# First MLP's late part: three tiles of 512 tokens become two of 768, one of them with block sums for both weights

## The chip, the cores and the metric

The kernel runs on one core of one Trainium2 chip. The metric is device time in microseconds (us), the median of three timed runs. The traced execution has a time of its own, which stands beside its span.

## The reference, cut to what matters

Windowed attention (4 batches, 8 heads, 576 positions, head size 64), then two MLPs over the 2304 tokens of its output, with 512 model columns and 2048 hidden columns, all in float32:

```
x  = attention(q, k, v)                      # (2304, 512); first 4 heads: window of 32, last 4: every 4th of 128
h  = x @ moe_w_in;   r = max(h, 0);  g = r*r;             x2 = g @ moe_w_out
h2 = x2 @ moe2_w_in; g2 = h2 / (1 + exp(-h2));            out = g2 @ moe2_w_out
```

## The kernel before, in words

**Numbers.** Every float32 operand of an MLP is split into a high part (rounded to the matmul's fp32r format) and a low part (the remainder). One product of two blocks is three matmuls: high by high, high by low, low by high.

**Tiles.** Before, the first MLP has tiles of 256, 256, 256, 512, 512 and 512 tokens, the second three of 768 (`TILES`, L38). The first three tiles run interleaved in `mlp` (L771): for each of 16 hidden blocks of 128, twelve matmuls of 256 columns with the first weights (L788 to L790), the activation, and twelve with the second weights (L836 to L838).

**Late part, before.** The three tiles of 512 run in `mlp2` (L908). For the first weights it uses seven products of block sums in place of eight products of blocks: a pair f of hidden blocks takes seven products (a11 b11, a12 b21, s1 t1, s2 t2, s3 t3, s4 b22, a22 t4), each of six matmuls of 256 columns (L936, 42 matmuls a pair). VectorE adds the products up (L952 to L960). The second weights are multiplied plainly: for each hidden block twelve matmuls of 512 columns (L990 to L992).

**Second MLP.** Its tiles of 768 run in `strassen` (L1054), which uses seven products for both weights, at half a tile (384 columns) a matmul: 8 pairs of 42 matmuls for the first weights (L1094), then 7 lists of 8 steps of six matmuls for the second (L1182). ScalarE moves a product out of PSUM (L1070), VectorE adds onto it (L1065); before the second weights each block of g, or a difference of two of them (L1162), is split by ScalarE (high, L1169) and VectorE or GpSimd (low, L1171) into an `hl` buffer.

**Weights.** Weights arrive as 64-bit numbers and are converted to float32 on ScalarE, VectorE and GpSimd (`weights`, L255). `sums` (L362) makes the block sums of first weights and writes them to DRAM, `sums2` (L403) those of second weights, before only for the second MLP. `stream` and `stream2` read them back. `load_x` (L856) and `load_xs` (L1009) read a tile of x and make its blocks and block sums.

**Attention.** 32 blocks (8 halves of a batch by 4 pairs of heads). The 8 earliest leave the division for later (`late_exp`, L680). Of these the first `AHEAD` subtract the row maximum from the scores on VectorE or GpSimd (`less`, L691, L694) and are then transposed plainly (L713); the others have it subtracted on TensorE, by one extra matmul behind each transpose (L715, L717).

**Order.** Nothing is scheduled at run time. `ORDER` is a table of some 4000 words, written in advance by a planner with costs and due times (the constants at the end of the file); a word such as `V1531` puts operation 1531 next in VectorE's queue (P TensorE, A ScalarE, V VectorE, G GpSimd, D SyncE's DMA queue, F fillers that keep TensorE busy). Each engine runs its queue in that order and waits where an operand isn't ready. All DMAs go through SyncE's queue.

Of the kernel before, what the change touches and what calls it, by code (L numbers as in the profile page):

```python
# [23 lines left out]
AHEAD = 4  # L24
# [3 lines left out]
P = 128  # L28
# [12 lines left out]
POOLS = {"u2": (8, 512), "u3": (2, 512), "u4": (28, 1024), "w1": (16, 1024), "blk": (BLK_BUFS, 1280)}  # L41
SHARED_LO = 91
SHARED_HI = 205
HOLDS = {"w0": "u4", "wa": "u4", "ws": "u4", "wb": "u4", "wc": "u2", "h": "u4", "xr": "u4", "xo": "u2", "cw": "u2", "raw": "u4", "ap": "u4", "x": "u4", "x2": "u4", "xn": "u2", "g4": "u4", "st": "u4",
         "g2": "u2", "cv": "u2", "r": "u3", "yo": "u2", "stg": "u2", "wp": "hi", "sq": "hi", "sw": "hi", "xq": "lo", "xs": "lo", "gq": "lo", "sg": "hi", "hl": "hi", "yq": "hi"}
# [132 lines left out]
class Kern:  # L178
# [76 lines left out]
    def weights(self, m, c, key, dkey, js=(0, 1)):  # L255
# [3 lines left out]
        for j in js:  # L259
# [5 lines left out]
                    self.spot("wp" if c < 2 * KEPT else "sq", 2 * wide, F32R) if late else self.buf("w1", NF, 2 * n, F32R))  # L265
# [54 lines left out]

            f = ((lambda b: b.tile.rearrange("p (a q n) -> p a q n", a=2, q=2)) if turn or split else
# [10 lines left out]
            if late:  # L332
                f = c // 2
                names = ("a12", "a22") if c % 2 else ("a11",)
                if f < KEPT:
                    for i, name in enumerate(names):
                        self.wp[name, f] = (Part(both, 512 * i, 256), Part(both, 512 * i + 256, 256), [h, r])
                else:
                    for i, name in enumerate(names):
                        self.kept[name, f] = self.op({"DMA": c_dma(P * n * 4)}, lambda e, both=both, f=f, name=name, i=i: nc.sync.dma_start(  # L340
                            out=self.w2y[PLAIN.index(name), f], in_=both.tile[:, 512 * i:512 * i + 512].bitcast(F32)), [h, r], k, [], [both])
                self.cv[c] = (cv, w)
                if c % 2:
                    self.sums2(f, k)
# [9 lines left out]
            else:  # L354
                self.wt[m, j, c] = (hi, lo, h, r)
                if m == j == 0:
                    half = lambda t: t.rearrange("p (q a n) -> p q a n", q=2, a=2)[:, :, 1]
                    self.kept[0, c] = self.op({"DMA": c_dma(P * n * (4 if c % 2 else 8))}, lambda e, both=both, c=c, half=half: nc.sync.dma_start(
                        out=self.w1s[c][:, :n].rearrange("p (q n) -> p q n", q=2) if c % 2 else self.w1s[c],
                        in_=half(both.tile.bitcast(F32)) if c % 2 else both.tile.bitcast(F32)), [h, r], k + W1_BACK, [], [both])  # L360

    def sums(self, f, key, m=1):  # L362

        nc = self.nc
        if m == 0:
            got = []
            for c in (2 * f, 2 * f + 1):
                b = self.spot("cw", PIECE)
                wh, wl, h, l = self.wt[0, 0, c]
                o = self.op({"Pool": c_pool2(PIECE), "DVE": c_dve(PIECE)}, lambda e, b=b, wh=wh, wl=wl: self.eng[e].tensor_tensor(  # L370
                    out=b.tile, in0=wh.tile.bitcast(F32), in1=wl.tile.bitcast(F32), op=ALU.add), [h, l], key, [b],
                    [wh, wl], f"c0.{c}", True)
                o.gate = key
                got.append((b, o))
            (ca, wa), (cb, wb) = got
# [27 lines left out]
    def sums2(self, f, key):  # L403

        nc = self.nc
        (ca, wa), (cb, wb) = self.cv[2 * f], self.cv[2 * f + 1]
# [6 lines left out]
        for i, (x, y, op) in enumerate(what):  # L413
# [5 lines left out]
                                + ([s[0]] if i == 3 else []), f"T{f}.{i}", True))  # L419
        for q in range(2):  # L420
            v = lambda i, q=q: s[q].tile.rearrange("p (i q n) -> p q i n", i=2, q=2)[:, i]
            h = self.op({"ACT": c_act(PIECE), "Pool": c_pool1(PIECE)}, lambda e, v=v: self.copy(e, v(0), v(1).bitcast(F32)),
                        [done[2 * q], done[2 * q + 1]], key, [], [s[q]], f"Th{f}.{q}")
            deps = [h] + ([done[3]] if q == 0 else [])
            r = self.op({"DVE": c_dve(PIECE), "Pool": c_pool2(PIECE)}, lambda e, v=v: self.sub(
                e, v(1), v(1).bitcast(F32), v(0).bitcast(F32)), deps, key, [], [s[q]], f"Tl{f}.{q}", True)
            o = self.op({"DMA": c_dma(P * PIECE * 8)}, lambda e, q=q: nc.sync.dma_start(
                out=self.w2y[2 * q:2 * q + 2, f].rearrange("i p n -> p i n"),
                in_=s[q].tile.bitcast(F32).rearrange("p (i n) -> p i n", i=2)), [h, r], key, [], [s[q]])
            for i in range(2):  # L430
                self.kept[f"s{2 * q + i + 1}", f] = o
# [6 lines left out]
    def stream(self, m, f, key, whole):  # L438
# [16 lines left out]
        n = 512 if whole else 1024  # L455
        b, o = load("wc" if whole else "wb", src[:, :n], n, deps, 0.1)
        out["a22"] = (Part(b, 0, 256), Part(b, 256, 256), o)
        if not whole:
            out["a21"] = (Part(b, 512, 256), Part(b, 768, 256), o)
        else:  # L460
            for j in range(2):
                b, o = load("ws", (self.w1x, self.w2x)[m][f, j], 1024, [self.kept[m, f, "s"][j]], 0.2 + j)
                for i in range(2):
                    out[f"s{2 * j + i + 1}"] = (Part(b, 256 * i, 256), Part(b, 512 + 256 * i, 256), o)
        return out


    def stream2(self, name, f, key):
# [5 lines left out]
            in_=self.w2y[i, f:f + 2].rearrange("f p n -> p f n")), [self.kept[name, f], self.kept[name, f + 1]], key, [b])  # L474
        o.gate, o.behind, self.last_sw = key, self.last_sw, o
        for g in range(2):
            self.wp[name, f + g] = (Part(b, 512 * g, 256), Part(b, 512 * g + 256, 256), [o])

    def load_blk(self, h, pair, key):
# [11 lines left out]
        else:  # L491
            parts, o0 = [], 0
            for w, late in ((cq + ck, 0), (cv, V_LAG)):
                b = self.buf("w1", NF, 2 * PIECE)
# [276 lines left out]
    def mlp(self, m, tiles):  # L771
# [3 lines left out]
        for c, ti in sorted(((c, ti) for c in range(NF) for ti in range(len(tiles))), key=lambda x: tiles[x[1]][1](x[0])):  # L775
# [48 lines left out]
            wh, wl, dh, dl = self.wt[m, 1, c]  # L824
# [5 lines left out]
            def s2(e, c=c, gh=gh, gl=gl, wh=wh, wl=wl, n=n, ti=ti, yb=ybanks):  # L830
# [850 lines left out]
```

## Time and profile before

| what | value |
|---|---|
| timed runs, us | 849.41 median (848.76 to 850.98) |
| profiled execution | 851.04 us, span 849.3 us |
| TensorE (PE) busy | 840.2 us |
| VectorE (DVE) busy | 681.8 us |
| ScalarE (ACT) busy | 501.2 us |
| GpSimd (POOL) busy | 121.9 us |

Matmuls are pipelined, so the sum of their durations is larger than the time that they take: what one costs is the distance from its start to the next one's start. The same holds, less strongly, of VectorE and ScalarE, whose rows give a mean duration, and whose timeline gives starts. A row of the waits or the chain names what ended a wait.

### The profile page before, as it was taken

What the parts mean: (1) busy time and instruction counts of PE and PEld (TensorE: products, weight loads), DVE (VectorE), ACT (ScalarE), POOL (GpSimd) and SP (SyncE); (2) the same over time, 40 slices, a digit from 0 to 9 for tenths busy, and PEclk for the clock granted to TensorE, in tenths of its full rate; (3) what the DMA queues carried; (4) which work ended last, traced back from release to release, by engine and by line L of the source; (5) the groups of instructions that cost most, each with busy time, mean ns of one, the idle gap of its engine ahead of it and who ended that gap; (6) DMA issues with size and microseconds to landing.
All of it is one profiled execution on the core that took longest, in us unless ns stands there. A gap on an engine that the chain in (4) does not pass through costs nothing.

```text
span 849.3 us, 17021 instructions
## 1 busy us (share of the span) xinstructions
PE 840.2 (99%) x6009; PEld 796.2 (94%) x6009; DVE 681.8 (80%) x1754; ACT 501.2 (59%) x1324; POOL 121.9 (14%) x142
## 2 busy tenths in 40 slices
PE   8999999999999999999999999999999999999998
PEld 7879999999989889889998999999999999999998
DVE  5999999888888698768899998898735788437865
ACT  4999988888566255324543466575445555345652
POOL 2211000101210202131201002202200111201120
PEclk9999999999999999999999999999999999999999
DMA  9486558779888888998999999889774675871751
GB/s 343 164 281 221 152 188 319 257 275 333 317 293 305 315 286 286 335 318 278 332 348 313 324 315 357 298 282 319 248 266 149 240 262 168 269 265 41 243 159 65
DMA packets 83604, 223.56 MB, mean 263 GB/s; under 512 B 8768, under 2 KB 18240, under 8 KB 83520
## 3 DMA queue, kind: packets, MB, share of 16 engines
q1 hardware_dynamic: 83520, 222.49, 75.6%
q8 instruction: 47, 0.77, 0.3%
q14 instruction: 37, 0.30, 0.1%
HBM read 172.13 MB, written 50.33 MB: 262 GB/s over the span
## 4 chain that ended last, share of the span: by engine, by line
PE 94%; ACT 4%; DVE 1%; DMA 0%; issue 0%; POOL 0%; SPq 0%; POOLq 0%; ACTq 0%
PE y L1094 17%; PE sa L1182 15%; PE s L936 14%; PE y L1182 6%; PE y L990 5%; PE y L991 5%; PE y L992 5%; PE sa L1094 4%; PE s L788 3%; PE s L789 2%; PE s L790 2%; PE ax L533 2%; PE y L836 2%; PE ax L625 2%; PE y L837 2%; PE y L838 2%
## 5 line engine op out<-in xcount | busy, mean ns | idle before, releaser
L245 ACT CAST hl<-gq 128x384 fp32r<-128x384 f32 x168 | 79.5, 513 | 62.7 <-PE sa L1182 27.0
L1094 PE MATMUL y<-xs,ws 128*128 128x384 f32 x552 | 107.5, 334 | 0.0
L1094 PEld LDWEIGHTS y<-xs,ws 128*128 128x128 f32 x552 | 96.7, 188 | 0.1
L252 DVE TENSOR_TENSOR hl<-gq,hl 128x384 fp32r<-128x384 f32 x144 | 78.7, 581 | 17.6 <-ACT hl L245 14.5
L1070 ACT COPY gq<-y 128x384 f32<-128x384 f32 x92 | 42.6, 479 | 69.1 <-PE y L1094 61.7
L1182 PE MATMUL sa<-hl,wp 128*128 128x384 f32 x432 | 79.1, 334 | 0.0
L936 PE MATMUL s<-x,ws 128*128 128x256 f32 x576 | 76.2, 284 | 0.0
L990 PE MATMUL y<-g,w 128*128 128x512 f32 x192 | 76.2, 397 | 0.0
L952 DVE TENSOR_TENSOR h<-s,h 128x512 f32<-128x512 f32 x96 | 59.5, 621 | 20.8 <-PE s L936 17.4
L1182 PEld LDWEIGHTS sa<-hl,wp 128*128 128x128 f32 x432 | 75.3, 188 | 0.0
L991 PE MATMUL y<-g,w 128*128 128x512 f32 x192 | 75.2, 391 | 0.0
L992 PE MATMUL y<-g,w 128*128 128x512 f32 x192 | 74.9, 390 | 0.0
L245 ACT CAST g<-r 128x256 fp32r<-128x256 f32 (+1 forms) x86 | 42.9, 504 | 52.0 <-DVE r L972 46.0
L936 PEld LDWEIGHTS s<-x,ws 128*128 128x128 f32 x576 | 72.2, 191 | 1.2
L566 ACT ACTIVATE ap<-ap,ast 96x128 f32<-96x128 f32 (+3 forms) x168 | 62.2, 372 | 8.3 <-DVE ast L575 4.2
L1065 DVE TENSOR_TENSOR gq<-y,gq 128x384 f32<-128x384 f32 x46 | 25.0, 554 | 52.0 <-PE y L1094 45.7
L788 PE MATMUL s<-x,w 128*128 128x256 f32 x192 | 56.3, 293 | 0.1
L1133 DVE TENSOR_TENSOR gq<-gq,sg 128x768 f32<-128x768 f32 x48 | 46.9, 992 | 10.3 <-ACT sg L1131 10.3
L790 PE MATMUL s<-x,w 128*128 128x256 f32 x192 | 54.3, 283 | 0.0
L789 PE MATMUL s<-x,w 128*128 128x256 f32 x192 | 54.2, 282 | 0.0
L1182 PE MATMUL y<-hl,sw 128*128 128x384 f32 x288 | 51.4, 334 | 0.0
L1182 PE MATMUL sa<-hl,sw 128*128 128x384 f32 x288 | 50.9, 334 | 0.0
(177 smaller groups left out, 2123.6 us busy)
## 6 DMA issues: line engine op xcount, KB each, us to landing
raw<-w SPq DMA_DIRECT2D x64, 512.0 KB, 6.1
ws<-w1x SPq DMA_DIRECT2D x48, 512.0 KB, 6.4
ws<-w2x SPq DMA_DIRECT2D x48, 512.0 KB, 5.4
sw<-w2y SPq DMA_DIRECT2D x48, 512.0 KB, 4.6
wa<-w1s SPq DMA_DIRECT2D x24, 512.0 KB, 6.9
wa<-w2s SPq DMA_DIRECT2D x24, 512.0 KB, 5.8
w1x<-st SPq DMA_DIRECT2D x16, 512.0 KB, 5.2
w2x<-st SPq DMA_DIRECT2D x16, 512.0 KB, 4.4
```

Of the source, the lines that this page charges most:

```text
L245: self.nc.scalar.copy(out=out, in_=in_)
L252: self.eng[eng].tensor_tensor(out=out, in0=a, in1=b, op=ALU.subtract)
L566: es.append(self.op({"ACT": c_act(nk) + 0.185}, lambda e, i=i, n=n, c=c, p=p, st=st: nc.scalar.activation(out=p.tile[:n, c], in_=p.tile[:n ...
L788: nc.tensor.matmul(o, wh.tile[:, s], xh, start=(kk == 0), stop=False)
L789: nc.tensor.matmul(o, wh.tile[:, s], xl, start=False, stop=False)
L790: nc.tensor.matmul(o, wl.tile[:, s], xh, start=False, stop=(kk == KC - 1))
L936: nc.tensor.matmul(bank.tile[:, o:o + 256], wp, xp, start=i == 0, stop=last, skip_group_check=True)
L990: nc.tensor.matmul(o, wh.tile[:, s], gh.tile, start=c == 0, stop=False)
L991: nc.tensor.matmul(o, wh.tile[:, s], gl.tile, start=False, stop=False)
L992: nc.tensor.matmul(o, wl.tile[:, s], gh.tile, start=False, stop=(c == NF - 1))
L1094: nc.tensor.matmul(o, w[part == 2].tile[:, kk * P:kk * P + P], x[b][part == 1].tile[:, kk * half:kk * half + half], start=new and not kk a ...
L1182: nc.tensor.matmul(o, u.tile[:, c * P:c * P + P], v.tile, start=new and not q and not part, stop=q == nf - 1 and part == 2, skip_group_che ...
```

## The change

The first MLP's tiles become 256, 256, 256, 768 and 768. `load_x` and `mlp2` go; both late tiles run in `load_xs` and `strassen`, which get a branch for the first MLP's activation (`relu2`, on VectorE in one instruction or on ScalarE in two). The first tile of 768 uses seven products for the first weights alone, and then `whole`: twelve matmuls of 384 columns a hidden block and half tile. The second uses seven products for the second weights too; for that `sums2` also makes the block sums of the first MLP's second weights (recombined on the chip from high and low part by `again`), writes them to DRAM (`w1y`), and `stream2` reads them back. The first MLP's second weights are stored in halves of 256 columns (`second`). `AHEAD` falls from 4 to 1, buffers are laid out anew, and the order table and its constants are new. Attention and the second MLP compute as before.

```diff
-AHEAD = 4
+AHEAD = 1
-TILES = ([(0, 256), (256, 256), (512, 256), (768, 512), (1280, 512), (1792, 512)], [(0, 768), (768, 768), (1536, 768)])
+TILES = ([(0, 256), (256, 256), (512, 256), (768, 768), (1536, 768)], [(0, 768), (768, 768), (1536, 768)])
...
+            if m == 0 and j:
+                self.second(c, cv, w, k, at)
+                continue
...
+    def second(self, c, cv, w, k, at):
+        halves, deps = [], []
+        parts = 1 if c % 2 else 2
+        n = PIECE // parts
+        for i in range(parts):
+            both = self.buf(("w1", "w1o")[c % 2], (16, 8)[c % 2], 2 * n, F32R)
...
+            h = self.op({"ACT": c_act(n), "Pool": c_pool1(n), "DVE": c_dve2(n)}, lambda e, v=v, cs=cs: self.copy(e, v(0), cs()),
+                        [w], k, [both], [cv], "h" + at, True)
+            r = self.op({"DVE": c_dve(n), "Pool": c_pool2(n)}, lambda e, v=v, cs=cs: self.sub(
+                e, v(1), cs(), v(0).bitcast(F32)), [h], k, [], [cv, both], "l" + at, True)
...
-    def sums2(self, f, key):
+    def sums2(self, m, f, key):
-        (ca, wa), (cb, wb) = self.cv[2 * f], self.cv[2 * f + 1]
+        (ca, wa), (cb, wb) = (self.cv[2 * f], self.cv[2 * f + 1]) if m else [self.again(1, c, key, key - T_LATER) for c in (2 * f, 2 * f + 1)]
...
+    def again(self, j, c, key, gate):
...
+            for i, (wh, wl, d) in enumerate(self.wt[0, 1, c]):
+                o = self.op({"Pool": c_pool2(256), "DVE": c_dve(256)}, lambda e, i=i, wh=wh, wl=wl: self.eng[e].tensor_tensor(
+                    out=b.tile[:, 256 * i:256 * i + 256], in0=wh.tile.bitcast(F32), in1=wl.tile.bitcast(F32), op=ALU.add), d + [o], key,
...
-    def load_x(self, m, t, key):
...
-    def mlp2(self, m, t, k0, fetched):
...
-                        done["g", i, q] = self.op({"DVE": c_dve(n)}, lambda e, b=b: nc.vector.scalar_tensor_tensor(
-                            out=b.tile, in0=b.tile, scalar=0.0, in1=b.tile, op0=ALU.max, op1=ALU.mult), deps, k + 0.2, [], [b], None, True)
+                        done["g", i, q] = self.op({"DVE": c_dve(n), "ACT": 2 * c_act(n)}, lambda e, b=b: self.relu2(e, b), deps, k + 0.2, [], [b],
+                                                  f"u{m}.{t}.{q}.{i}", True)
...
+        if m == 0 and t in WHOLE:
+            return self.whole(m, t, k0, done, g, chain, lag)
...
+    def whole(self, m, t, k0, done, g, chain, lag):
...
+        for s in range(2):
+            yb = [self.bank(f"y{e}") for e in range(KC)]
...
+            for c in range(NF):
...
+                def s2(e, es, c=c, hi=hi, lo=lo, halves=halves, yb=yb):
+                    for ee in es:
+                        wh, wl, _ = halves[ee // 2]
+                        w = slice(ee % 2 * P, ee % 2 * P + P)
+                        for part, (u, v) in enumerate(((wh, hi), (wh, lo), (wl, hi))):
+                            nc.tensor.matmul(yb[ee].tile[:, :half], u.tile[:, w], v.tile, start=not c and not part,
+                                             stop=c == NF - 1 and part == 2, skip_group_check=True)
...
+        for f in range(NF // 2):
+            self.sums2(0, f, T_FROM + T_STEP * f + T_LATER)
+        big = [(0, t) for t in range(FIRST, len(TILES[0]))] + [(1, t) for t in range(len(TILES[1]))]
...
+    def relu2(self, e, b):
+        if e == "ACT":
+            self.nc.scalar.activation(out=b.tile, in_=b.tile, func=AF.Relu)
+            self.nc.scalar.square(out=b.tile, in_=b.tile)
...
+WHOLE = (3,)
```

## Rows read from the trace of the kernel before

**Rows 1.** The page's chain that ended last: shares of the span by engine.
```profile
PE 94%; ACT 4%; DVE 1%; DMA 0%; issue 0%; POOL 0%; SPq 0%; POOLq 0%; ACTq 0%
```
**Rows 2.** That chain by line, 220 to 350 us, then 350 to 485 us.
```profile
by line: PE s L936 42.5%; PE y L990 14.3%; PE y L991 13.4%; PE y L992 13.3%; PE ax L533 6.2%; PE ax L625 4.5%; PE ax L602 3.6%; PE zx L836 0.9%; PE zx L837 0.7%; PE zx L838 0.7%
...
by line: PE s L936 48.5%; PE y L990 16.9%; PE y L991 16.6%; PE y L992 16.5%; PE sa L1094 0.8%; PE ax L625 0.5%; PE ax L602 0.4%
```
**Rows 3.** Windows of 25 us: busy us (and instructions) of each engine.
```profile
core 0: us, PE busy (x) PEld busy (x) DVE busy (x) ACT busy (x) POOL busy (x), PEclk, DMA share, GB/s
25.00:50.00 25.00, 23.58 (x220) 21.55 (x221) 24.30 (x99) 24.46 (x78) 4.41 (x5) 1.00 0.49 157
50.00:75.00 25.00, 23.73 (x264) 21.85 (x263) 24.26 (x107) 23.28 (x78) 4.00 (x5) 1.00 0.88 301
75.00:100.00 25.00, 25.00 (x237) 23.59 (x236) 23.98 (x92) 23.66 (x80) 1.40 (x2) 1.00 0.41 118
425.00:450.00 25.00, 25.00 (x162) 22.84 (x161) 24.03 (x46) 12.13 (x24) 0.99 (x1) 1.00 0.96 330
475.00:500.00 25.00, 25.00 (x143) 22.50 (x142) 24.49 (x44) 12.10 (x23) 1.96 (x2) 1.00 0.88 302
```
**Rows 4.** Pieces of the chain: start us, length us, what (L936 256, L1182 384 columns).
```profile
164.94 0.67 PE ax L625 x12
...
208.74 0.83 PE ax L533 x12
...
419.91 8.63 PE s L936 x72
...
571.15 8.32 PE sa L1182 x48
```
**Rows 5.** PE's timeline, 512 columns: first and last of 14 matmuls, and what follows.
```profile
439.79 0.39 PE L991 MATMUL y<-g,w 128*128 128x512 f32 x1
...
442.74 0.39 PE L992 MATMUL y<-g,w 128*128 128x512 f32 x1
442.97 1.59 PE L936 MATMUL s<-x,wa 128*128 128x256 f32 x12
```
**Rows 6.** Groups of matmuls by line: count | busy us, mean ns | idle before.
```profile
L936 PE MATMUL s<-x,ws 128*128 128x256 f32 x576 | 76.2, 284 | 0.0
L990 PE MATMUL y<-g,w 128*128 128x512 f32 x192 | 76.2, 397 | 0.0
L936 PE MATMUL s<-x,wa 128*128 128x256 f32 x288 | 40.9, 286 | 0.0
L936 PE MATMUL s<-x,wc 128*128 128x256 f32 x144 | 21.2, 283 | 0.0
```
**Rows 7.** PE's timeline: plain transposes, of three and of four units, and what follows.
```profile
13.40 0.42 PE L713 MATMUL ax<-ident,ap 96*128 96x96 f32 x3
13.65 0.53 PE L738 MATMUL ax<-w,ap 96*96 96x65 f32 x4
...
16.04 0.41 PE L713 MATMUL ax<-ident,ap 72*72 72x72 f32 x4
16.35 0.49 PE L1248 MATMUL fill<-warm 128*128 128x256 bf16 x3
```
**Rows 8.** PE's timeline: transposes with the extra matmul, three units, then four.
```profile
24.93 0.27 PE L715 MATMUL ax<-ident,ap 96*128 96x96 f32 x1
...
25.82 0.36 PE L788 MATMUL s<-x,w 128*128 128x256 f32 x1
...
53.54 0.27 PE L715 MATMUL ax<-ident,ap 72*104 72x72 f32 x1 [0.20 <-DVE w L247]
...
54.66 0.55 PE L625 MATMUL ax<-ap,blk 96*64 96x96 f32 x8
```
**Rows 9.** VectorE's subtractions of the row maximum, by line.
```profile
L691 DVE TENSOR_TENSOR ap<-ap,ast 72x288 f32<-72x288 f32 (+2 forms) x10 | 3.4, 376 | 0.0
```
**Rows 10.** VectorE's timeline: starts in a row at 256, 512, 768 and 384 columns.
```profile
435.56 0.42 DVE L417 TENSOR_TENSOR st<-cv 128x256 f32<-128x256 f32 x1
435.90 0.42 DVE L417 TENSOR_TENSOR st<-cv,st 128x256 f32<-128x256 f32 x1
...
440.25 0.69 DVE L972 SCALAR_TENSOR_TENSOR r<-h 128x512 f32<-128x512 f32 x1
440.85 0.69 DVE L311 SCALAR_TENSOR_TENSOR cv<-raw,cv 128x512 int32<-128x512 int32 x1
...
547.49 0.96 DVE L1133 TENSOR_TENSOR gq<-gq,sg 128x768 f32<-128x768 f32 x1 [0.72 <-ACT sg L1131]
548.37 0.55 DVE L252 TENSOR_TENSOR gq<-gq 128x384 f32<-128x384 f32 x1
548.84 0.55 DVE L1065 TENSOR_TENSOR gq<-y,gq 128x384 f32<-128x384 f32 x1
```
**Rows 11.** ScalarE's timeline: exponentials; PSUM move, split, two sigmoids, split.
```profile
162.10 0.34 ACT L566 ACTIVATE ap<-ap,ast 72x72 f32<-72x72 f32 x1
162.34 0.19 ACT L566 ACTIVATION_READ_ACCUMULATOR ap<-ap,ast 72x1 f32 x1
162.44 0.34 ACT L566 ACTIVATE ap<-ap,ast 72x72 f32<-72x72 f32 x1
...
558.71 0.48 ACT L1070 COPY gq<-y 128x384 f32<-128x384 f32 x1 [0.47 <-PE y L1094]
559.09 0.52 ACT L245 CAST hl<-gq 128x384 fp32r<-128x384 f32 x1
559.50 1.58 ACT L1131 ACTIVATE sg<-gq 128x768 f32<-128x768 f32 x2
560.98 0.50 ACT L245 CAST hl<-gq 128x384 fp32r<-128x384 f32 x1
```
**Rows 12.** Groups on VectorE and ScalarE by line: count | busy us, mean ns | idle before.
```profile
L252 DVE TENSOR_TENSOR hl<-gq,hl 128x384 fp32r<-128x384 f32 x144 | 78.7, 581 | 17.6 <-ACT hl L245 14.5 <-POOL hl L252 2.7
L566 ACT ACTIVATE ap<-ap,ast 96x128 f32<-96x128 f32 (+3 forms) x168 | 62.2, 372 | 8.3 <-DVE ast L575 4.2 <-DVE ast L558 3.7
L1133 DVE TENSOR_TENSOR gq<-gq,sg 128x768 f32<-128x768 f32 x48 | 46.9, 992 | 10.3 <-ACT sg L1131 10.3
L566 ACT ACTIVATION_READ_ACCUMULATOR ap<-ap,ast 72x1 f32 (+1 forms) x168 | 31.8, 189 | 0.0
```

More of the change, by code (lines that the diff above doesn't have):

```diff
@@ L355, in weights @@
                 self.wt[m, j, c] = (hi, lo, h, r)
[L356 to L360, printed above, removed]
+                half = lambda t: t.rearrange("p (q a n) -> p q a n", q=2, a=2)[:, :, 1]
@@ L365, in sums @@
         if m == 0:
[L366 to L375, printed above, removed]
+            (ca, wa), (cb, wb) = [self.again(0, c, key, key) for c in (2 * f, 2 * f + 1)]
         else:
@@ L436, in f32, with stream @@
         return t if t.dtype == F32 else t.bitcast(F32)
-    def stream(self, m, f, key, whole):
+    def stream(self, m, f, key):
         nc = self.nc
@@ L454, in stream, with stream2 @@
         src, deps = own(2 * f + 1)
-        n = 512 if whole else 1024
-        b, o = load("wc" if whole else "wb", src[:, :n], n, deps, 0.1)
+        b, o = load("wc", src[:, :512], 512, deps, 0.1)
         out["a22"] = (Part(b, 0, 256), Part(b, 256, 256), o)
[L458 to L464, printed above, removed]
+        for j in range(2):
+            b, o = load("ws", (self.w1x, self.w2x)[m][f, j], 1024, [self.kept[m, f, "s"][j]], 0.2 + j)
+            for i in range(2):
+                out[f"s{2 * j + i + 1}"] = (Part(b, 256 * i, 256), Part(b, 512 + 256 * i, 256), o)
         return out
-    def stream2(self, name, f, key):
+    def stream2(self, m, name, f, key):
         b = self.spot("sw", 1024, F32R)
@@ L838, in s2 @@
                     nc.tensor.matmul(o, wl.tile[:, s], gh.tile, start=False, stop=(c == NF - 1), **kw)
-            prev[t] = self.op({"PE": 12 * c_mm(n)}, s2, [dh, dl, hi, lo, prev.get(t), first], k2, al,
-                              [wh, wl, g] + ([] if al else use))
+            prev[t] = self.op({"PE": 12 * c_mm(n)}, s2, [hi, lo, prev.get(t), first] + halves[0][2] + halves[1][2], k2, al,
+                              [p[0] for p in halves] + [g] + ([] if al else use))
             first = first or prev[t]
@@ L1009, in load_xs @@
+                o = self.op({"DMA": c_dma(P * n * 4)}, lambda en, yo=yo, dst=dst, t0=t0, n=n:
+                            nc.sync.dma_start(out=dst[:, t0:t0 + n], in_=yo.tile), [a], key(NF + 1), [], [yo])
+                self.ydone.append((m, e, t0, t0 + n, o))
     def load_xs(self, m, t, key):
@@ L1101, in strassen @@
                 chain.pace = name == "A1"
+                if q == nf - 1 and name == LAG:
+                    lag = chain
                 k = key + 0.1
@@ L1278, in run @@
             k = W2_FROM + W2_STEP * c if c < W2_SPLIT else end + W2_LATE + W2_LSTEP * (c - W2_SPLIT)
-            self.weights(1, c, k, k - 4, (0,))
+            self.weights(1, c, k + LATER, k - 4, (0,))
         for c in range(NF):
             k = end + W2B_FROM + W2B_STEP * c
-            self.weights(1, c, k, k - 4, (1,))
-        ahead = lambda m, t: [self.stream(m, f, start(m, t) + 2 * unit[m][t] * (f - W_AHEAD), TILES[m][t][1] == 512)
-                              for f in range(NF // 2)]
@@ L1285, in run @@
[L1285 to L1304 removed]
+            self.weights(1, c, k + LATER2, k - 4, (1,))
@@ L1614 @@
+P4247 A4238@202 A4248 D4239 D4249
 """
```

890 lines of the change are left out of this document (419 added, 471 removed).

## The prediction, made before the change was run

> **What bounds the kernel now.** I read the chain of work that ended last, then the windows, then the timelines of the engines. The chain is TensorE's for 94% of the span and ScalarE's and VectorE's for 5% [rows 1]. That 6% is not TensorE's makes some 0.06 x 849.3 = 51 us, and they lie early: between 220 and 485 us every line of the chain is TensorE's [rows 2], and the windows show TensorE below 25 of 25 us only before 75 us, with VectorE and ScalarE at 23.3 to 24.5 us there [rows 3]. So there are two regimes. Up to some 75 us attention and the conversion of weights set the pace, and TensorE is on the chain for about a third (75 - 51 = 24 us). From there to the end TensorE has always something ready, at a granted clock of 1.00 (its upper level, 2.4 GHz) in each window shown [rows 3]. A busy TensorE is no proof, since durations overlap; the chain is. The late part of the first MLP, which the change rewrites, lies wholly in the second regime: there a matmul less is time less, as long as the others keep up. VectorE is the one to watch: 24.03 and 24.49 of 25 us busy at 425 and 475 us, and the chain still was TensorE's [rows 2, 3].
>
> **The change, part by part.**
>
> *TensorE, late part.* Prices first, by starts. 256 columns: 72 matmuls in 8.63 us, 0.1199 us each; 384 columns: 48 in 8.32 us, 0.1733 us [rows 4]. 512 columns: 14 from 439.79 to 442.97 us, 0.2271 us [rows 5]. Removed: 576 + 288 + 144 = 1008 matmuls of 256 columns for the first weights and 3 x 192 = 576 of 512 columns for the second [rows 6]: 1008 x 0.1199 + 576 x 0.2271 = 120.9 + 130.8 = 251.7 us. Added: for the first weights 2 tiles x 8 pairs x 42 = 672; for the second in `whole` 2 halves x 16 blocks x 12 = 384, with seven products 7 x 8 x 6 = 336. That is 1392 matmuls of 384 columns, x 0.1733 = 241.2 us. Term: **-10.4 us**. The first weights stay at 258,048 columns, with fewer instructions; the second weights lose an eighth of one tile's work.
>
> By the rows a matmul costs its columns at 2.4 GHz (106.7, 160.0, 213.3 ns) and 13 to 14 ns more [rows 4, 5], so that 192 fewer matmuls are worth 2.6 us of the 10.4. The Trainium skill's page "TensorE: Matmul & The Clock Gate", section "Back-to-back issue gap", gives 2.5 ns for that excess in an isolated stream; by it, as an estimate, the term would be -8.2 us. The rows decide; nothing below uses the page's figure.
>
> *TensorE, attention.* With `AHEAD` 1 the blocks 1, 2 and 3 get the extra matmul behind each transpose. A plain transposition of three units takes 0.25 us and of four 0.31 [rows 7]; with the extra matmul three take 25.82 - 24.93 = 0.89 and four some 54.66 - 53.54 = 1.1 [rows 8]. Two halves a block: 2 x 0.64 + 4 x 0.8 = 4.5 us more work, all in the first 30 us, where TensorE is on the chain for a third. Bounds: 0 if hidden in those waits, 4.5 if not; a third is 1.5. Against it, VectorE and GpSimd lose six subtractions, 6 x 0.376 = 2.3 us [rows 9], of which something between 0 and 2.3 comes back; VectorE is the smaller part of the chain [rows 1], so I take 0.5. Term: **+1.0 us**.
>
> *First MLP's second weights in halves.* The even blocks are split in two pieces of 256 columns, not one of 512. On VectorE that is 2 x 0.34 - 0.60 = 0.08 us for each of 8 blocks [rows 10], under 1 us over the first 75 us; ScalarE's pieces cost as little. I counted the words of both order tables up to the first matmul of a late tile and priced them by starts: VectorE has 188 us of work there before and 190 after, ScalarE 174 and 179, against some 200 of TensorE. So the first regime should end about where it did. Taken as 0, bounds -3 and +5.
>
> *VectorE and ScalarE, late part.* `sums2` for the first MLP adds, for each of 8 pairs, 4 recombinations and 4 sums of 256 and 2 remainders of 512 columns: 8 x (8 x 0.34 + 2 x 0.60) = 31 us [rows 10], a fifth of it on GpSimd in the table. The second weights' seven products add splits and differences, `mlp2`'s additions (L952) and products (L972) go. By the tables VectorE has 1527 words before and 1597 after, ScalarE 1092 and 1223, GpSimd 123 and 108. Priced by starts, VectorE's whole work grows by 14 us and ScalarE's by 75, mostly activations (23 of 32 `relu2`) and splits. What matters is where. The fullest stretch for VectorE is the second weights of the tile with both products and the first weights of the second MLP's first tile: TensorE has 112 steps of 1.04 us = 116.5 us there [rows 4], and the table gives VectorE 111 operations of 384 columns, 23 of 768, 29 sums of 256, 47 passes of 512 over weights and sums, and 15 small ones: 111 x 0.47 + 23 x 0.88 + 29 x 0.34 + 47 x 0.60 + 15 x 0.34 = 115.6 us. It is full, yet not over. The nearest rows are the stretches at 94 to 98% of before, where the chain stayed TensorE's [rows 2, 3]. Taken as **0**; the other end, by mean durations, is below.
>
> *DMA.* Both tables hold 516 transfers. Streams of first weights shrink from 24 to 16 pairs of 1.75 MB (42 to 28 MB); block sums of second weights add 8 MB each way. Work that TensorE's chain never showed; 0.
>
> *Ends.* The second MLP's three tiles and the last copy are as before: 0.
>
> **Sum.** -10.4 + 1.0 = -9.4 us. The profiled span of 849.3 would become 839.9, its own time of 851.04 some 841.6; the runs' median of 849.41 becomes **840.0 us**.
>
> **The rivals.**
>
> 1. *VectorE becomes the bound in that full stretch, and the kernel is slower.* If its instructions don't overlap, because each one waits for ScalarE's split, they cost their mean durations, 0.58 and 0.99 in place of 0.47 and 0.88 [rows 10, 12]. Then the 116.5 us of TensorE's work need about 111 x 0.57 + 23 x 0.98 + 29 x 0.42 + 47 x 0.69 + 15 x 0.43 = 136.9 us of VectorE: +20.4 us, 860.4 us. It decides from a price halfway between: at +9.4 us the gain is gone. For it: VectorE's splits did wait 14.5 us for ScalarE in all [rows 12], and the table leaves half of that tile's splits about one step (1 us) ahead of their matmuls. Against it: starts at 0.47 us in the same code [rows 10].
>
> 2. *ScalarE becomes the bound over the first weights of the first tile of 768.* The last attention blocks fall there too. TensorE: 56 steps of 1.04, 4 steps of 1.44 and attention (8 scores at 0.83, 14 transpositions at 0.25, 7 products at 0.66), together 79 us [rows 4, 7]. ScalarE by the table: by starts (0.34 an exponential with its read, 0.38 a move, 0.74 a pass of 768 [rows 11]) some 66 us; by durations (0.56, 0.48, 0.85 [rows 11, 12]) 87 us, 8 more than TensorE. Price 0 to +8, so up to 848 us.
>
> 3. *The first regime gets shorter or longer.* It is 75 us of waits in a new order; 51 us of them aren't TensorE's [rows 1]. Shorter by a tenth: 835 us. Longer by a tenth: 845 us.
>
> 4. *The gain is hidden anyway:* TensorE waits as long as it saves at one of the new seams, where `whole` and the next tile use the same four accumulator banks twice; three steps of 0.52 us cover each copy of 0.48 us, so I see no place for it. 849 us.
>
> **How the numbers follow.** What a measurement of this kernel can tell from no change is 0.3%, 2.5 us. Forecast, TensorE stays the bound (837 to 843 us): 0.57. Rival 3: shorter 0.10 (834 to 837), longer 0.05 (843 to 846). Rival 2 or a mild form of rival 1 (843 to 849): 0.13, of which 0.06 lies within 0.3%. Rival 4: 0.05. Rival 1 in full (over 852): 0.10. Faster: 0.57 + 0.15 + 0.07 = 0.79; same 0.06 + 0.05 = 0.11; slower 0.10. The range of 835 to 849 us leaves out rival 1 in full, half of rival 4 and the edge of the shorter start, together under 0.2.
>
> **What would show it.** In the profile after: 1392 matmuls of 384 columns in place of L936 and L990 to L992, at 0.173 us from start to start; the chain all TensorE's from some 75 us on; first matmul of the second MLP's first tile some 9 us earlier; VectorE at 24 of 25 us around the tile with both products, without waits of TensorE for `hl`. Wrong would be: waits of TensorE for VectorE's splits there (rival 1), for ScalarE's moves in the first 768 tile (rival 2), or an end of the first regime shifted by more than 3 us.

## The result, and the profile after

The changed kernel took 854.45 us (853.92 to 855.52, 4 runs) beside 849.31 us for the kernel before: a ratio of 1.0058, 95% interval 1.0041 to 1.0075. It is slower by 0.6%, where 840.0 us was forecast. Timed once more, beside the experiments (run e6 below), it took 852.33 us to 849.33: 1.0028 (1.0011 to 1.0044). Its dozen runs there lie between 847.4 and 854.4 us, the 35 of the kernel before between 848.3 and 852.5. The granted clock over the whole run was 0.996 to 0.998 in three of the first four runs, and 0.998 in four of the later twelve.

The page's chain that ended last, by engine, and a piece of the chain (start us, length us, what), both of the changed kernel; they answer to [rows 1] and [rows 4]:

```profile
PE 86%; DMA 7%; DVE 4%; ACT 2%; issue 1%; SPq 0%; DVEq 0%; ACTq 0%
```

```profile
626.19 6.24 PE y L976 x36
```

The price of a matmul of 384 columns is as forecast, 6.24/36 = 0.1733 us. But 7% of the chain are transfers now, where it was 0%.

Windows of the changed kernel, to be read beside [rows 3], with three stretches more:

```profile
core 0: us, PE busy (x) PEld busy (x) DVE busy (x) ACT busy (x) POOL busy (x), PEclk, DMA share, GB/s
75.00:100.00 25.00, 25.00 (x240) 23.35 (x239) 24.65 (x108) 24.76 (x97) 2.45 (x4) 1.00 0.69 218
175.00:200.00 25.00, 21.91 (x191) 21.08 (x190) 20.77 (x74) 17.74 (x55) 3.44 (x4) 0.95 0.86 301
200.00:225.00 25.00, 25.00 (x217) 24.49 (x216) 18.99 (x41) 14.26 (x42) 1.45 (x3) 0.91 0.72 250
475.00:500.00 25.00, 24.94 (x141) 23.92 (x140) 24.44 (x45) 17.73 (x35) 1.02 (x1) 1.00 0.97 343
500.00:560.00 60.00, 59.04 (x332) 57.03 (x331) 57.26 (x106) 46.10 (x88) 9.90 (x10) 1.00 0.93 332
```

The view that says most is the shortest: what TensorE waited for between 75 and 560 us (us in total, times, longest us; stops of 0.15 us and less are left out). For the kernel before it holds no line at all. For the changed one:

```profile
PE zx L870 <- ACT g L245: 2.2, 1, 2.2
PE y L976 <- DMA ws<-w1x: 2.0, 2, 1.5
PE s L821 <- DVE ast L591: 0.9, 1, 0.9
PE ax L635 <- ACT xo L245: 0.8, 1, 0.8
PE y L976 <- ACT gq L952: 0.6, 2, 0.4
PE y L976 <- DVE gq L947: 0.6, 2, 0.3
PE y L976 <- DMA wa<-w1s: 0.4, 1, 0.4
```

Together 7.5 us. Followed back, some 5 of them end on a transfer (2.2, 2.0, 0.4 and 0.4 of the waits for `gq` behind ScalarE), the rest on work in VectorE's or ScalarE's queue (0.9, 0.8 and the other waits for `gq`). The longest is put down to ScalarE. Its own timeline, the chain's pieces and TensorE's timeline at this place tell another story:

```profile
194.23 0.39 ACT L245 CAST g<-r 128x256 fp32r<-128x256 f32 x1
197.50 0.41 ACT L245 CAST g<-r 128x256 fp32r<-128x256 f32 x1 [2.88 <-DMA y<-yo]
```

```profile
190.08 7.40 DMA y<-yo
...
202.35 0.21 PE s L821
202.57 0.21 PE s L822
...
205.69 0.12 PE y L871
205.80 0.12 PE y L872
```

```profile
194.85 0.94 PE L566 MATMUL ax<-blk 64*72 64x104 f32 x16
197.96 0.58 PE L870 MATMUL zx<-g,w1o 128*128 128x256 f32 x1 [2.17 <-ACT g L245]
```

ScalarE's data was there, but the place that the order table gives to its output `g` still held a copied `yo` block, and the store of that block took 7.40 us to land. After the stop the matmuls start 0.21 us apart, not 0.12, up to 205 us: the granted clock had fallen to its lower level, as the 0.95 and 0.91 of the two windows say. The stop and the slower matmuls cost some 2.2 + 3.4 us (the clock's record has 6.8 us at half speed).

The same pattern further on, in two stretches of the chain:

```profile
396.79 9.65 DMA w2x<-st
...
406.45 5.82 DMA ws<-w1x
```

```profile
504.86 1.28 DVE cv L318 x2
...
509.78 4.91 DMA w2y<-st
...
514.79 0.49 ACT gq L952
```

A load waits for the store that empties its place, then needs 5.82 us itself; ScalarE's move out of PSUM waits for a store likewise. That second store was issued late: the pieces of the chain left out between 504.86 and 509.78 us are VectorE's, with 0.9 us of issue, so VectorE's queue and the landing stand one behind the other there. The longest stop for a load, 1.5 us, has no store behind it:

```profile
300.10 1.06 PE y L976 x6
...
301.18 4.45 DMA ws<-w1x
...
305.67 1.49 PE y L976 x7
```

Here the place came free with TensorE's own last matmul on it, and the load's 4.45 us were longer than the other work at hand.

Landing times themselves are no news of the changed kernel. Loads of the same block sums, before and after (times issued, KB each, median us from issue to landing):

```profile
ws<-w1x SPq DMA_DIRECT2D x48, 512.0 KB, 6.4
```

```profile
ws<-w1x SPq DMA_DIRECT2D x32, 512.0 KB, 6.2
```

What is new is which work stands behind them.

An account, worked out from TensorE's starts in both traces (an instruction's own price is the lower quartile of the time to the next start for the same pair of shapes in both, what is above it is lost time): matmuls outside attention cost 742.1 us before and 731.2 after, **-10.9**; lost time behind them 11.0 and 20.3, **+9.3**; attention with its lost time and the fillers 91.3 and 97.4, **+6.0**. The sum is the difference of the spans (853.7 - 849.3 = 4.4). The trace of the second timing, e6, gives -10.9, +8.1 and +3.4 by the same account (span 849.9).

### The profile page after: what moved, and what is told of

Read it like the earlier page. It is cut to its first block, busy times and chain, and to the rows that moved or that the text cites. A ratio compares the mean times of both kernels' runs of the same rounds, so it can differ in the third digit from the quotient of the medians.

```text
span 853.7 us, 16986 instructions
## 1 busy us (share of the span) xinstructions
PE 837.5 (98%) x5859; PEld 811.4 (95%) x5859; DVE 690.7 (81%) x1823; ACT 578.5 (68%) x1475; POOL 100.6 (12%) x120
## 4 chain that ended last, share of the span: by engine, by line
PE 86%; DMA 7%; DVE 4%; ACT 2%; issue 1%; SPq 0%; DVEq 0%; ACTq 0%
PE y L976 25%; PE sa L1068 18%; PE y L1068 8%; PE y L1134 8%; PE sa L976 4%; PE s L821 3%; PE ax L566 2%; PE s L822 2%; PE s L823 2%; DMA raw<-w 2%; PE y L870 2%; PE y L871 2%; PE y L872 2%; PE ax L658 2%; PE ax L635 1%; DMA w2y<-st 1%
## 5 line engine op out<-in xcount | busy, mean ns | idle before, releaser
L976 PE MATMUL y<-xs,ws 128*128 128x384 f32 x960 | 187.6, 336 | 2.6 <-DMA ws<-w1x 2.0
L245 ACT CAST hl<-gq 128x384 fp32r<-128x384 f32 x256 | 120.7, 511 | 79.1 <-DVE gq L252 24.5
L976 PEld LDWEIGHTS y<-xs,ws 128*128 128x128 f32 x960 | 167.3, 188 | 4.8 <-DMA ws<-w1x 2.5
L252 DVE TENSOR_TENSOR hl<-gq,hl 128x384 fp32r<-128x384 f32 x240 | 129.1, 569 | 22.3 <-ACT hl L245 21.7
L1068 PEld LDWEIGHTS sa<-hl,sw 128*128 128x128 f32 x384 | 66.6, 188 | 0.7 <-DVE hl L252 0.7
L1068 PEld LDWEIGHTS y<-hl,sw 128*128 128x128 f32 x384 | 66.6, 188 | 0.4 <-ACT hl L245 0.4
L252 DVE TENSOR_TENSOR gq<-gq 128x384 f32<-128x384 f32 x123 | 65.5, 556 | 0.9 <-POOL hl L252 0.7
L976 PE MATMUL y<-xs,wc 128*128 128x384 f32 x240 | 49.3, 339 | 0.7 <-DVE gq L947 0.6
L976 PE MATMUL y<-xs,wa 128*128 128x384 f32 x240 | 48.8, 337 | 0.4 <-DMA wa<-w1s 0.4
L976 PE MATMUL sa<-xs,wa 128*128 128x384 f32 x240 | 48.4, 336 | 0.0
```

The lines of the kernel that those rows point to most:

```text
L245: self.nc.scalar.copy(out=out, in_=in_)
L252: self.eng[eng].tensor_tensor(out=out, in0=a, in1=b, op=ALU.subtract)
L976: nc.tensor.matmul(o, w[part == 2].tile[:, kk * P:kk * P + P], x[b][part == 1].tile[:, kk * half:kk * half + half], start=new and not kk a ...
L1068: nc.tensor.matmul(o, u.tile[:, c * P:c * P + P], v.tile, start=new and not q and not part, stop=q == nf - 1 and part == 2, skip_group_che ...
```

## The experiments

Two theories first. **Landing:** TensorE loses time where a place in memory comes free only when a transfer has landed. **Full VectorE:** it loses time because VectorE has 24 to 25 of 25 us between 425 and 560 us (rival 1 in a mild form). A third question is the attention term. Every run: median us, ratio to the kernel before timed beside it with its 95% interval, and the sum of TensorE's waits between 75 and 560 us by the same view as above. The waits are those of one profiled run each; the run of e11 took 856.3 us, its other eleven 845.1 to 848.1 (why, in the last section).

| run | median | ratio | interval | waits |
|---|---|---|---|---|
| changed kernel, first | 854.45 | 1.0058 | 1.0041-1.0075 | 7.5 |
| e6_after_again | 852.33 | 1.0028 | 1.0011-1.0044 | 7.0 |
| e1_places | 848.50 | 0.9994 | 0.9981-1.0007 | 6.1 |
| e2_no_w1y | 850.94 | 1.0026 | 1.0010-1.0042 | 5.4 |
| e3_no_differences | 850.48 | 1.0015 | 1.0005-1.0025 | 4.7 |
| e5_after_less | 856.98 | 1.0102 | 1.0081-1.0122 | 4.8 |
| e4_before_minus | 850.98 | 1.0019 | 1.0009-1.0028 | 0 |
| e7_places2 | 848.67 | 0.9986 | 0.9972-1.0001 | 5.7 |
| e8_places3 | 849.61 | 1.0002 | 0.9986-1.0017 | 5.2 |
| e9_relief | 847.08 | 0.9968 | 0.9956-0.9979 | 3.9 |
| e10_no_readd | 848.46 | 0.9989 | 0.9979-0.9998 | 5.7 |
| e11_all | 846.68 | 0.9976 | 0.9956-0.9997 | 3.8 |
| e12_no_sums_moved | 845.92 | 0.9951 | 0.9936-0.9967 | 4.0 |
| e13_order | 848.41 | 0.9983 | 0.9968-0.9998 | 5.4 |
| e14_best | 847.61 | 0.9968 | 0.9954-0.9982 | 5.0 |
| e15_gpsimd | 856.02 | 1.0069 | 1.0048-1.0090 | 10.2 |
| e16_after_gpsimd | 858.21 | 1.0106 | 1.0093-1.0120 | 11.8 |

**Four buffers at other places** (words of the order table; the number behind @ is the place):

```diff
-A1467@8    D2570@92  D2569@116  A2902@113
+A1467@116  D2570@8   D2569@92   A2902@141
```

> The changed kernel (854.45 us) with four buffers at other places of the memory, places that had been empty for 8 to 36 us: the high half g of the early tile's unit 2.7 no longer where a y store has still to land, two first-weight loads of the last first-MLP tile no longer where sum stores have to land, one split of that tile's second product likewise. Nothing else is moved. Landing theory (TensorE loses time where a buffer's place comes free only when a store has landed): the 2.2 us stop at 195 us goes, with the lowered clock that followed it (up to 3.4 us), and the 0.5 and 0.7 us stops at 405 and 411 us: 3 to 7 us less, 847.5 to 851.5. Full-VectorE theory (the loss is that VectorE has 24 to 25 of 25 us between 425 and 560 us): those stops stay, at most 2 us less, 852.5 to 854.5.

5.9 us less than the first measurement of the changed kernel and 3.8 less than the second: the landing theory's range, and nothing but places was changed. The interval lies clear of both measurements of the changed kernel, so its slowness against the kernel before is gone with four places; the forecast gain has not come. Followed matmul by matmul, the trace of e1 gains 6.1 us on the first trace, 3.5 of them between 195 and 205 us, and 2.3 us on that of e6, 1.4 of them between 400 and 425 us, where moved loads stand. Its windows from 175 to 225 us have a granted clock of 1.00, but the stop near 195 us is not gone. VectorE's timeline:

```profile
194.99 0.17 DVE L608 RECIPROCAL ast<-ast 72x4 f32<-72x4 f32 x1
197.01 0.26 DVE L591 CUSTOM_DVE_ANT_0 ap<-ax,mask 72x104 f32<-72x104 f32 x1 [1.86 <-DMA w2x<-st]
```

Attention's buffer `ap` lay where another store had still to land; it costs TensorE 1.5 us in place of 2.2. In the first trace VectorE waited for ScalarE's `g` up to 197.94 us, so that this store didn't show.

**The second weights' block sums of the first MLP not moved:**

```diff
-lambda e, q=q: nc.sync.dma_start(
+lambda e, q=q: m and nc.sync.dma_start(
...
-self.wp0[name, f + g] = (Part(b, 512 * g, 256), Part(b, 512 * g + 256, 256), [o])
+self.wp0[name, f + g] = self.wp0["a22", f + g]
```

> The changed kernel without the 16 stores and 16 loads of the second weights' block sums (16.8 MB between 95 and 490 us); the four products that used them read a resident block in their place, so that part of the output is not computed; every sum is still formed, every product still made. Landing theory: transfers land sooner and the sums' buffers come free at once, stops behind DMA from 175 to 500 us go, 4 to 8 us less, 846.5 to 850.5. Full-VectorE theory: VectorE's work is the same, 0 to 1.5 us less, 853 to 854.5.

**VectorE's differences left out:**

```diff
-lambda e, p=p, o=o, u=u, v=v: self.sub(e, p(o), p(u), p(v))
+lambda e, p=p, o=o, u=u, v=v: self.sub(e, p(o), p(u), p(v)) if m or e == "Pool" else None
```

> The changed kernel without the 31 differences that VectorE forms of the last first-MLP tile's hidden activations (the second product then reads undifferenced blocks, so that part of the output is not computed): 16 to 17 us of VectorE's time between 430 and 500 us gone, DMA unchanged. Full-VectorE theory: TensorE's short stops between 425 and 560 us go, 3 to 4.5 us less, 850 to 851.5. Landing theory: these stops end on buffers and loads, VectorE only follows, 0 to 1.5 us less, 853 to 854.5.

By the first measurement these two gave 3.5 and 4.0 us, and each theory would have had its number. So the changed kernel was timed again.

> The changed kernel as it is, timed once more beside the others: 854.5 us, with stops of TensorE near 195 us of 2 to 3 us in each run and a granted clock below 1.0 in some of its runs. If it comes out near 850, most of what the versions with one part undone gained was the difference between chips, and their gains are to be read against this run.

It came out between the two numbers expected. In its trace the stop near 195 us is shorter, and the granted clock stayed at 1.00 (a piece of e6's chain, and a row of its timeline):

```profile
189.70 6.38 DMA y<-yo
```

```profile
196.56 0.38 PE L870 MATMUL zx<-g,w1o 128*128 128x256 f32 x1 [0.74 <-ACT g L245]
```

The same store in the same place, landed 1 us sooner, cost 0.74 us and no lowered clock. So in this stretch the trace of e1 gains nothing on that of e6.

Against e6, the two versions gave 1.4 and 1.9 us. Neither is clear of noise, since their intervals overlap that of e6, and part of even that lies elsewhere: of e3's span, 7.0 us shorter than the changed kernel's in its profile, 4.3 were gained before 275 us, where the two are the same. In the stretch itself VectorE was relieved, and TensorE gained nothing (windows of the kernel before, of the changed kernel, then of e3):

```profile
425.00:500.00 75.00, 75.00 (x447) 67.46 (x446) 70.90 (x126) 31.54 (x58) 6.27 (x8) 1.00 0.93 324
500.00:560.00 60.00, 60.00 (x347) 59.86 (x346) 52.74 (x95) 38.79 (x75) 9.71 (x10) 1.00 0.90 317
```

```profile
425.00:500.00 75.00, 74.80 (x425) 72.97 (x424) 72.43 (x145) 57.13 (x111) 3.05 (x3) 1.00 0.94 330
```

```profile
425.00:500.00 75.00, 74.68 (x424) 72.89 (x423) 60.89 (x115) 56.64 (x112) 3.06 (x3) 1.00 0.96 342
500.00:560.00 60.00, 59.42 (x337) 57.91 (x336) 58.07 (x111) 46.82 (x89) 9.89 (x10) 1.00 0.94 327
```

From 425 to 500 us VectorE is 11.5 us less busy, and TensorE as it was; by the account above its lost time there is 1.9 and 2.0 us. The full-VectorE theory, as stated, falls for 425 to 500 us.

**The attention term**, both ways round: the subtractions put back into the changed kernel, and dropped from the kernel before. (What these texts call the row minimum is that of the negated scores: the row maximum.)

```diff
-AHEAD = 1
+AHEAD = 4
...
-P40@3
+V4252 P40@3
```

> The changed kernel with the subtraction back in the first four pairs of attention (VectorE subtracts the row minimum before the transpose, plain transposes) as the kernel before has it; everything behind is as changed. Prediction's term: 1.0 us less, 853.5. If TensorE's extra 4.5 us are on the path in full: 850. If the start is bound by what the first loads bring: no change, 854 to 855, with the stops before 75 us longer by what the transposes are shorter.

```diff
-AHEAD = 4
+AHEAD, SUBTRACT = 4, 1
...
-V40 V51 V72 V83 V103 V114
+
```

> The kernel before with one part of the change alone: the six subtractions of the row minimum in pairs 1 to 3 of the first half are dropped and TensorE adds the minimum in the transpose's bank, as it already did for pairs 4 to 7; TensorE's order and all else are as before. Prediction's term: 4.5 us more TensorE work of which 1.0 shows, 850.1 us. If TensorE is the bound there throughout: 853.6. If the start waits for the first loads and for VectorE: 849.1 or less.

In the kernel before the part costs 1.65 us by the medians, 0.8 to 2.4 by the interval, so 1.0 isn't ruled out. Putting it back into the changed kernel made that slower, by 2.5 us or more: the six words were set right before the transposes and VectorE came late (TensorE waits 2.9 us for `ap` at the new subtractions), and the clock fell, in all six runs (0.984 to 0.989 over the run), as its windows show:

```profile
0.00:25.00 25.00, 20.68 (x176) 16.46 (x176) 16.20 (x103) 13.49 (x39) 5.67 (x16) 0.80 0.77 274
25.00:50.00 25.00, 24.07 (x181) 22.21 (x182) 20.35 (x79) 18.89 (x60) 2.67 (x4) 0.73 0.72 242
```

It says little on the term and much on how tight the start is.

**More places, and a load moved up:**

```diff
-P978@1@0@36@3  D2275@80  A3093@100  A3111@154
+P978@1@0@96@3  D2275@55  A3093@154  A3111@100
```

> The version with four moved buffers (848.5 us) with four more: the attention scores' buffer of pair 5.3 no longer where a sum store has still to land, the last block-sum load of the first 768-token tile to a place that comes free one product earlier, two of the second MLP's hidden blocks with their places exchanged. Landing theory: the 1.65 us stop that was left at 196.6 us goes, a part of the 1.2 us at 299.5 us and of the 0.9 us at 526 us: 2 to 3.5 us less, 845 to 846.5. Full-VectorE theory: 848 to 848.5.

```diff
-D1869
+D2997@108 D1869
...
-D2997@120 D3000@108
+D3000@120
```

> The version with eight moved buffers, and one load of the second MLP's block sums issued ahead of three stores that wait for VectorE in the same queue, at a place that is free 6 us earlier (its follower takes the old place). Landing theory: the 0.9 us stop at 526 us goes too: 844.5 to 846. Full-VectorE theory: 848 to 848.5, as VectorE's work is the same.

Both missed: 848.67 and 849.61 us, no better than four places. The 1.5 us stop at 197 us did go, but others of its size came, at a load of attention's next block (1.5 us) in e7 and at VectorE's `gq` (1.6 us in two) in e8. The same kernel's other stops change from run to run, so a place mended for one trace is worth less than that trace's stop.

**The reliefs together, and VectorE's adding again dropped** (e9: the diffs of e2 and e3 on top of e7; e10: the sums read the high half, of which one line is shown, and the additions are dropped; e11: both):

```diff
-a = lambda i, j: Part((ca, cb)[i], 256 * j, 256)
+a = lambda i, j: Part((ca, cb)[i], 256 * j, 256) if m else Part(self.wt[0, 0, 2 * f + i][0], 256 * j, 256)
```

> The version with eight moved buffers (848.7 us), and with the block sums of the first MLP's second weights neither stored nor loaded and VectorE's 31 differences of the last first-MLP tile left out, as in the two runs before (those parts of the output are not computed). Alone these two gave 1.4 and 1.9 us against the changed kernel timed beside them (852.3). If the causes add up: 845 to 845.5. If VectorE, the transfers and the places each wait for the others, so that taking away one leaves the rest as the bound: 842 to 844. If they are all the same stops: 847 to 848.7.

> The version with eight moved buffers (848.7 us), with the block sums of the first MLP's weights formed from the high halves alone: VectorE doesn't add high and low half again (29 additions, some 16 us of VectorE between 105 and 330 us; the low halves' share of the sums is left out). If VectorE's full queue makes the stops between 145 and 300 us (0.85, 1.05, 1.65 and 1.2 us): 2 to 3 us less, 845.5 to 846.7. If transfers and places make them: 848 to 848.7.

> All of the two runs beside it together: eight moved buffers, no transfers of the second weights' block sums, no differences, no adding again. If the dozen stops of 0.2 to 1.7 us behind the first 75 us, 9 us in the traces, come from VectorE's queue, the transfers and the places together: 840 to 843.5. If something else makes them (ScalarE, the order of TensorE's work): 845 or more.

Of what e9 allowed for, 847.1 us fits "the same stops": 1.6 us less than e7, where adding up would have given 3 to 4. Of what e11 allowed for, "something else" holds: with all reliefs 846.7 us, only 2.0 less than with the places alone, and the adding again by itself 0.2. Where the time stops in e10 is seen in rows of its timeline (SyncE, then TensorE twice) and in a piece of its chain:

```profile
478.66 0.32 SPq L483 DMA_DIRECT2D wa<-w2s  x1
...
484.40 1.30 PE L976 MATMUL y<-xs,wa 128*128 128x384 f32 x6 [1.47 <-DMA wa<-w2s]
...
544.72 1.11 PE L976 MATMUL y<-xs,ws 128*128 128x384 f32 x5 [1.35 <-DMA ws<-w2x]
```

```profile
534.02 10.57 DMA ws<-w2x
```

Both stops, 1.47 and 1.35 us, are for a load of weights that was issued 5.7 and 10.6 us before its first matmul. VectorE has a part in the first: SyncE issues its transfers in order, and what it waited for between 470 and 480 us, ahead of that load, was

```profile
SPq L465 <- DVE st L252: 3.4, 1, 3.4
SPq L483 <- DMA w2y<-st: 2.6, 1, 2.6
```

VectorE's sums for the next store, and then a store that had to land.

**Neither MLP's block sums moved (e12, on top of e9; its diff isn't shown); the order on two engines (e13; e14 adds the dropped additions):**

```diff
-V2134@88        A1382 ... A859@12
+V2438 V2134@88  A859@12 A1382
```

> The version with eight moved buffers, without the differences, and with neither MLP's block sums of the second weights stored or loaded (resident blocks are read in their place, so those products are not computed): some 33 MB of transfers less from 410 us to the end, beside the 8 MB before that. Against the run with only the first MLP's left out (847.1 us): if the full transfer queue makes the stops that are left between 410 and 560 us, 3 us: 844 to 845. If the order of work on VectorE and ScalarE or TensorE's own order makes them: 846.5 to 847.1.

> The version with eight moved buffers (848.7 us) with two instructions moved up in the order table and nothing else: VectorE's split of the hidden half 0.3.0.10 ahead of the block sums of the second weights that stood before it in its queue, and ScalarE's copy of an attention output ahead of a square. If the order on these engines makes the stops at 147 us (0.85 us) and 326 us (0.6 to 1.3 us): 847 to 848. If not, 848.7.

> The version just named, with the block sums of the first MLP's weights formed from the high halves alone and all 48 instructions that add high and low half again dropped, VectorE's and GpSimd's (the low halves' share of the sums is left out). If VectorE's queue is a part of what is left: 846 to 847.5, faster than the kernel before by 0.2 to 0.4%. If transfers alone are: 848.

Windows of e12:

```profile
425.00:500.00 75.00, 74.97 (x430) 74.16 (x429) 62.51 (x119) 56.83 (x113) 3.06 (x3) 1.00 0.56 192
500.00:560.00 60.00, 58.98 (x337) 57.78 (x336) 57.19 (x108) 46.34 (x89) 9.93 (x10) 1.00 0.69 231
```

The waits for loads between 410 and 560 us are gone with the transfers, and TensorE has 74.97 of 75 us in the first stretch; the time is 1.2 us under e9's, where 2 to 3 were expected. From 500 us little changed: VectorE still has 57.19 of 60, where the kernel before has 52.74, and TensorE's lost time by the account is 2.2 us, where the kernel before has 0.2. In e13 the split moved up took its stop away (e7's wait of 0.4 us for VectorE's `hl` at 327 us is gone from the view), the copy moved up did not (0.8 us for `xo` stays), and the time stayed within what can be told. e14 is faster than the kernel before, by 0.3%; of its gain over e13, 0.8 us, little can be told from none.

**VectorE's work to GpSimd from 495 to 545 us:**

```diff
-V1987 V1995 V1997 V1989 V2021 V2015 V2023 V2047 V2049 V2065 V2041 V2067 V2073 V2075
+G1987 G1995 G1997 G1989 G2021 G2015 G2023 G2047 G2049 G2065 G2041 G2067 G2073 G2075
```

> The fastest version so far that leaves only the low halves' share of the sums out (847.6 us), with eight additions and six shifts of the second MLP's second weights moved from VectorE to GpSimd in the order table, 8 us of VectorE's 57 between 495 and 545 us. If VectorE's full queue makes the stops of the second MLP's first tile: 1.5 to 2.5 us less, 845 to 846. If transfers or places do: 847.3 to 848.

> The changed kernel (852.3 us timed again) with the same 14 instructions moved from VectorE to GpSimd and nothing else. If VectorE's full queue makes the stops of the second MLP's first tile: 850 to 851. If not: 852 to 853, or slower where GpSimd's longer additions hold up the weights.

Some 8 and 6 us slower. Window and GpSimd's group in e15, VectorE's group for the same line in the changed kernel, and two of VectorE's waits in e15 between 495 and 545 us:

```profile
500.00:560.00 60.00, 53.71 (x289) 50.80 (x288) 49.69 (x84) 40.94 (x77) 25.27 (x22) 0.97 0.82 282
```

```profile
L318 POOL TENSOR_TENSOR cv<-cv,raw 128x512 int32<-128x512 int32 x8 | 12.3, 1549 | 10.3 <-ACT gq L952 3.3 <-DVE st L455 2.8 <-DVE gq L1017 1.8
```

```profile
L318 DVE CUSTOM_DVE_ANT_0 cv<-raw,cv 128x1024 uint16<-128x1024 uint16 x60 | 40.7, 683 | 1.1 <-ACT sg L1015 0.5
```

```profile
DVE cv L314 <- POOL raw L304: 3.5, 4, 1.2
DVE st L455 <- POOL cv L318: 2.4, 1, 2.4
```

VectorE is 7.6 us less busy there than in e14, from which e15 departs (57.33 us), and TensorE 5.5 (59.23). An addition takes 1549 ns on GpSimd, against 683 on VectorE, and what follows on VectorE, in order, waits for it; e14 has no such wait. The Trainium skill, page "GPSIMD Engine Reference", section "4.1 Engine selection", puts two-input elementwise work there at about twice VectorE's time. The trace agrees roughly, with 2.3, though the two engines do this addition by different instructions. The runs tell that latency counts in this stretch; whether VectorE's fullness does, they don't tell, since they brought a new wait.

## Why the prediction was wrong, by its own steps

*TensorE, late part: right.* Forecast -10.4 us; by starts the matmuls outside attention are 10.9 us cheaper.

*DMA, "Work that TensorE's chain never showed; 0": this step failed.* It counted bytes and transfers, which did stay much the same (222.5 and 224.6 MB in the two traces), and not what waits for them. The view of the kernel before shows no wait of TensorE between 75 and 560 us, that of the changed one 7.5, some 5 of them behind stores and loads that land 4 to 10 us after issue, mostly at a DMA share of 0.86 to 0.97. By the account, lost time behind matmuls, forecast as 0, is +9.3 us in the first trace and +8.1 in e6's. That places are a part of it is shown by e1: four places, nothing else, 3.8 to 5.9 us. With the transfers of the block sums and the differences gone as well (e12) it is 6.4 us less than the second measurement, about half of the way to 840.0. The order table's places belong to the change, and the prediction costed the table's words and never asked when the place that each word names comes free. The lowered clock behind the stop at 195 us, 3.4 us in the first trace and nothing in e6's, was no term at all.

*VectorE and ScalarE, "Taken as 0": right for 425 to 500 us, open from 500 to 560.* Rival 1 named the stretch; relieving VectorE by 11.5 us between 425 and 500 us moved TensorE's share by nothing, and e3 as a whole gave 1.9 us, not all of it from there. Behind 500 us no run relieved VectorE without bringing a new wait, so a mild form of rival 1 stands untested there. VectorE and ScalarE are also links of the waits: a split behind sums that wait for ScalarE (e13), a copy behind a store, a store behind VectorE's sums. Of rival 2, a wait for ScalarE's moves over the first weights of the first 768 tile, the view shows nothing; at rival 4's seams, the ends of the two halves of `whole` at 343 and 379 us, it shows no wait either. (The prediction's "stretches at 94 to 98%" are 96 and 98% in [rows 3].) Against 840.0 us e12 has the fewest causes left, and it is still 5.9 us above.

*TensorE, attention:* +1.0 forecast, +1.65 alone (e4), which agrees within its interval. In the changed kernel attention with its lost time and the fillers is +6.0 us in the first trace, where the lowered clock is a part of it, and +3.4 in e6's: 2 to 5 us more than the term. No run isolates that; e5, made for it, brought waits of its own.

*First regime, "should end about where it did":* the first matmul of a late tile starts at 225.2 us, not 217.5, and 221.2 in e6, later by 7.7 and 3.7 us, where the prediction named more than 3 as a sign of being wrong; part of it is attention that the new table puts earlier (280 of its instructions are left behind that point, not 360). The second MLP's first matmul comes at 489.8 us (486.9 in e6), not 9 us earlier than the 482.2 of the kernel before.

The rest is not settled. Some 6 to 8 us lie between e12, e14 (845.9, 847.6 us) and the forecast. The account tells where they are in e12, whose span of 844.7 us is 4.8 above the 839.9 forecast: lost time behind matmuls is 5.0 us more than before the change, 2.7 of it between 225 and 345 us and 2.0 between 500 and 560. In their traces these are stops of 0.2 to 1.2 us: two that stand in every run (0.8 us at 148 us for `xo`, 0.9 near 190 us for a PSUM bank that VectorE still reads), those at 500 to 560 us, and others that change place with each run. That no single relief brought them back fits loads and splits that are only just in time all along; no run shows it. A table made anew for the measured landing times would test it; it was not tried.

## What to carry to other kernels

Before you cost a transfer at nothing, list for every buffer what held its place last and when that use ends; where it is a store, its landing and not its issue frees the place. Where it is a load into a place that TensorE itself empties, compare the landing time with the work that is left until the data is needed. Where TensorE waits for nothing while VectorE and the transfers are at some 95%, a change that saves matmuls asks all loads and places to come earlier by as much; here they did not. Time a version with one part undone beside the changed kernel: the first comparison here made two reliefs look 2 us larger than the second, and even that one was between two chips. And look at more than one trace of a kernel: the longest stop of the first was a third as long in the second.

## What the runs showed of the hardware

Transfers on which TensorE's stops hung, of 128 to 512 KB, landed 4.5 to 10.6 us after issue, most of them at a DMA share of 0.86 to 0.97 (rows above). Under less load they land sooner: of the 512 KB loads `raw` between 425 and 500 us the median took 6.4 us in e7, at a share of 0.97, and 4.8 in e12, at 0.56; of the loads `wa` 8.6 and 5.6. The Trainium skill, page "DMA: Bandwidth & Descriptors", section "Latency and other measured facts", has the access to HBM rise from 0.2 us on average to 2 us at high load. The direction agrees; the rows are of whole transfers in a full queue and not of one access, so the sizes can't be compared.

The clock fell to its lower level for 6.8 us at the end of a stop of 2.2 us, behind another of 0.9; stops of 1.5 us in e1, e7 and e10 were not followed by a fall. In e15 it fell as well (0.97 in its window above). In e5 it stayed low over a good part of the first 50 us (0.80 and 0.73 of full speed as means), where the changed kernel, with more TensorE work in that start, kept 1.00. That is no safe level, though: the profiled run of e11, whose start is as in the changed kernel, has 0.91 and 0.68 in the same two windows, and was 9 us behind the first trace of the changed kernel at 50 us.
